# A filter copy and two transpose copies moved between engines, and the last filter products queued earlier, in a tuned FFT-mixing and FFN kernel

## The chip, the cores and the metric

The kernel runs on one core of one Trainium2 chip. The time is device microseconds (us) of one execution. "Span" is the time from the first to the last instruction in the profile, some 2 us shorter. Kernels that are compared were run in the same rounds on the same chip, unless the text says that they come from other rounds. A ratio is the mean time of one kernel's fast runs over that of the other's of the same rounds, so it isn't quite the ratio of the medians that are quoted.

TensorE is PE in the profile, VectorE DVE, ScalarE ACT, GpSimd POOL and SyncE SP.

## The reference

```
batch, seq, dim = 8, 3008, 256
X = rfft(x, axis=1); Y = X * (filt_r + 1j*filt_i); y = irfft(Y)     # per channel: mix along seq
x = y.reshape(24064, 256)
xn = x / rms(x) * rms_g
out = (silu(xn @ w_gate) * (xn @ w_val)) @ w_out                    # d_ff = 1536
```

The program calls one of the eight sequences a "channel". Channel 0 is transformed alone at the start. The other seven are transformed in small pieces between the FFN's matmuls of the channel before.

## The kernel before

Only the filter stage of channel 0, about 17 to 40 us, is concerned. In it 32 frequencies are handled in 16 *units* of two. A unit is a matmul into a PSUM bank (`b_mm`, called `stage_b`), two products with the filter (`b_unit`, called `products`), and the inverse matmuls (`bit_unit`, called `inverses`). Two units form a *pair*: their inverses accumulate in two banks, and the second one ends with two copies to `gT`.

```
# filter tables: four blocks fr[0..3], fi[0..3] of eight frequencies, loaded into half of the
# partitions; f_dup copies the other half: by ScalarE (A), GpSimd (G) or a SyncE transfer (S)
def f_dup(c, e, eng, lo=0, hi=KC):
    t = (fr, fi)[e][c][:, lo:hi, :]
    ...
    if eng is nc.scalar: eng.activation(out=t[a:a + HALF], in_=t[o:o + HALF], func=AXT.Copy)
    elif eng is nc.sync: eng.dma_start(t[a:a + HALF], t[o:o + HALF])
    else:                eng.tensor_copy(out=t[a:a + HALF], in_=t[o:o + HALF])

def t1_copy(g, on_act):          # group g of eight transposes, PSUM -> SBUF
    if on_act: nc.scalar.activation(out=dst, in_=ps[0:KR], func=AXT.Copy)
    else:      nc.vector.tensor_copy(out=dst, in_=ps[0:KR])

def b_unit(b, i, ps):            # products of unit i: VectorE, but units 3, 7, 9, 12 on GpSimd,
    ...                          # after ScalarE has copied the bank to v (GpSimd reads v)

def bit_unit(i):                 # inverses of unit i
    if not closing:
        st[0]["g"][pair] = [bank((3 * dh) if pair == 7 else (1 + dh), "pgt") for dh in range(2)]
    ...                          # 8 matmuls a unit, half of them for each of the two banks
    if closing: ...              # two copies pgt -> gT, mostly by ScalarE

# the schedule; in the traces each engine's instructions stand in this order
for g in range(4):
    t1_mm(g); t1_copy(g, g % 2)
stage_b(0, 1, 2, 3)
for g in range(4, 8): t1_mm(g)
t1_copy(4, 0)
f_dup(0, 0, A, 0, 2); f_dup(0, 1, G, 0, 2); f_dup(0, 0, A, 2, 4); f_dup(0, 1, G, 2, 8)
f_dup(0, 0, A, 4, 8)
products(0) ... products(1) ... t1_copy(5, 1); f_dup(1, 1, G); products(3)
f_dup(1, 0, A, 0, 4); f_dup(1, 0, A, 4, 8)        # "the block-1 copy" below
inverses(0, 1); products(2); t1_copy(6, 0); t1_copy(7, 0)
... # units 4 to 9
inverses(4); products(8); stage_b(12)
inverses(5)
f_dup(3, 1, A, 0, 4); products(12); w_load(0); w_load(1); products(10)
stage_b(13, 14); inverses(6); f_dup(3, 1, A, 4, 8); inverses(7)
... # units 8 to 15, then transposes, norm and FFN
```

Of the kernel before, what the change touches and what calls it, by code (L numbers as in the profile page):

```python
# [121 lines left out]
def kernel(  # L122
# [121 lines left out]
    def b_unit(b, i, ps=None):  # L244
        if ps is None:
            ps = b_mm(b, i)
        f1, f2 = filt(2 * i, 2)
        if b:
            s1 = late_p["sp"].tile([P, 2, D], FP16, tag="s1", name="s1")
            s2 = late_p["sp"].tile([P, 2, D], FP16, tag="s2", name="s2")  # L250
            if summed(b, i):
                nc.vector.tensor_tensor(out=s1, in0=ps, in1=f1, op=ALU.mult)  # L252
                st[b]["s"][i] = (s1, s2, ps, f2)
                return
        elif i % 2:
            s1 = hp.tile([P, 512], FP16, tag="sg", name="sg").rearrange("p (a d) -> p a d", a=2)
            s2 = hhs[(i // 2) % 4].rearrange("p (a d) -> p a d", a=2)
        else:
            ss = xnp.tile([P, 2, 512], FP16, tag="xn", name="ss")
            s1, s2 = (ss[:, e, :].rearrange("p (a d) -> p a d", a=2) for e in range(2))  # L260
        eng = nc.vector
        if (i in (3, 5, 8, 12, 15)) if b else (i in (3, 7, 9, 12)):
            eng = nc.gpsimd
            v = yp.tile([P, 2, 512], FP32, tag="y", name="v")
            v = v[:, 0, :].rearrange("p (a d) -> p a d", a=2)
            nc.scalar.activation(out=v, in_=ps, func=AXT.Copy)
            ps = v
        eng.tensor_tensor(out=s1, in0=ps, in1=f1, op=ALU.mult)
        eng.tensor_tensor(out=s2, in0=ps, in1=f2, op=ALU.mult)  # L269
        st[b]["s"][i] = (s1, s2)  # L270
# [241 lines left out]
    def f_dup(c, e, eng, lo=0, hi=KC):  # L512
        t = (fr, fi)[e][c][:, lo:hi, :]
        a, o = (0, HALF) if e else (HALF, 0)
        if eng is nc.scalar:
            eng.activation(out=t[a:a + HALF], in_=t[o:o + HALF], func=AXT.Copy)  # L516
        elif eng is nc.sync:
            eng.dma_start(t[a:a + HALF], t[o:o + HALF])
        else:
            eng.tensor_copy(out=t[a:a + HALF], in_=t[o:o + HALF])  # L520
# [13 lines left out]
    def t1_mm(g):  # L534
        if g < 6:
            if g % 2 == 0:
                st[0]["t2t"] = t2p.tile([KR, KC, D], FP16, tag="t2", name="t2")
            dst = st[0]["t2t"][:, 4 * (g % 2):4 * (g % 2) + 4, :]
        else:
            dst = t3p.tile([KR, 4, D], FP16, tag="t3", name="t2")  # L540
        st[0]["t2"][g] = dst
        pool, tag = ((psG, "pg"), (psV, "pv"))[g % 2]
        ps = pool.tile([P, 4, D], FP16, tag=tag, name="pt1")
        af = aT.rearrange("p a k -> p (a k)")
        for a in range(4):
            for dh in range(2):
                b0 = dh * H * P
                src = af[:, b0:b0 + 32 * P].rearrange("p (i k) -> p k i", k=K2)[:, 4 * g + a, :]
                nc.tensor.transpose(ps[:, a, ts(dh, P)], src, ident)
        st[0]["t2ps"][g] = ps  # L550

    def t1_copy(g, on_act):
        dst, ps = st[0]["t2"][g], st[0]["t2ps"].pop(g)
        if on_act:
            nc.scalar.activation(out=dst, in_=ps[0:KR], func=AXT.Copy)
        else:
            nc.vector.tensor_copy(out=dst, in_=ps[0:KR])

    def bit_unit(i):
        s1, s2 = st[0]["s"].pop(i)  # L560
        pair = i // 2
        closing = pair in st[0]["g"]
        if not closing:
            st[0]["g"][pair] = [bank((3 * dh) if pair == 7 else (1 + dh), "pgt") for dh in range(2)]
        for u in range(2):
            k = 2 * i + u
            for dh in range(2):
                o = st[0]["g"][pair][dh][:, ts(2 * (i % 2) + u, KR)]
                nc.tensor.matmul(o, s1[:, u, ds(dh * P, P)], wi_at(0, k)[:, 0:KR], start=True, stop=False)
                nc.tensor.matmul(o, s2[:, u, ds(dh * P, P)], wi_at(1, k)[:, 0:KR], start=False, stop=True)  # L570
        if closing:
            for dh in range(2):
                dst = gT[:, dh, pair * 4 * KR:(pair + 1) * 4 * KR]
                src = st[0]["g"][pair][dh][:, 0:4 * KR]
                if pair > 5 and dh:
                    nc.vector.tensor_copy(out=dst, in_=src)
                else:
                    nc.scalar.activation(out=dst, in_=src, func=AXT.Copy)  # L578
# [47 lines left out]
    def w_load(q):  # L626
        cols = ts(q, DFF // 3)
        for src, dst in ((moe_w_gate, wg), (moe_w_val, wv)):
            nc.gpsimd.dma_start(dst[:, :, cols], src.rearrange("(dt p) j -> p dt j", p=P)[:, :, cols])
        nc.gpsimd.dma_start(wo[:, ts(q, JT // 3), :],  # L630
                            moe_w_out.rearrange("(jt p) d -> p jt d", p=P)[:, ts(q, JT // 3), :])

    with tc.manual_schedule():
# [48 lines left out]
        A, G, S = nc.scalar, nc.gpsimd, nc.sync  # L682
        st[0]["t2ps"], st[0]["g"], psb = {}, {}, {}

        def products(*units):
            for i in units:
                b_unit(0, i, psb.pop(i))

        def stage_b(*units):
            for i in units:  # L690
                psb[i] = b_mm(0, i)

        def inverses(*units):
            for i in units:
                bit_unit(i)

        for g in range(4):
            t1_mm(g)
            t1_copy(g, g % 2)
        stage_b(0, 1, 2, 3)  # L700
        for g in range(4, 8):
            t1_mm(g)
        t1_copy(4, 0)
        f_dup(0, 0, A, 0, 2)
        f_dup(0, 1, G, 0, 2)
        f_dup(0, 0, A, 2, 4)
        f_dup(0, 1, G, 2, 8)
        f_dup(0, 0, A, 4, 8)
        products(0)
        stage_b(4)  # L710
        products(1)
# [23 lines left out]
        inverses(4)  # L735
        products(8)
        stage_b(12)
        inverses(5)
        f_dup(3, 1, A, 0, 4)
        products(12)  # L740
        w_load(0)
        w_load(1)
        products(10)
        stage_b(13, 14)
        inverses(6)
# [181 lines left out]
```

## Time and profile before

| | before |
|---|---|
| median time | 889.63 us (three runs, 889.43 to 890.09) |
| span of the profiled run | 886.7 us |
| filter stage | 17.6 to 40.4 us, PE busy 17.60 of 22.80 us |
| start of the block-1 copy on ScalarE | 24.97 us |
| first FFN matmul | 47.20 us |

After the first FFN matmul TensorE has practically no gap (from 110 to 860 us it is busy for 748.86 of 750.00 us).

```profile
47.20 0.38 PE L443 MATMUL pg<-xn,wg 128*128 128x512 f16 x1
```

The line above, from TensorE's instructions in order of time, is the kernel before's first FFN matmul (start, length, line, operation). The prediction shows the other lines.

### The profile page before, as it was taken

To read this page: it belongs to the slowest core of one execution; us is meant where nothing else is said; L and a number is where in the kernel's file an instruction comes from. 1 tells how busy PE (TensorE), PEld (TensorE's weight loads), DVE (VectorE), ACT (ScalarE), POOL (GpSimd) and SP (SyncE) were. 2 spreads that over 40 slices of the span, in tenths; PEclk is the share of its full clock that TensorE was granted. 3 is DMA by queue.
4 is the path that set the end of the run, shared out by engine and by line. 5 is a ranking of instruction groups with operands and counts; after the bars stand their busy time and mean duration, and the time that the engine had idled before them with its cause. 6 is when DMAs were issued, how large, how long until landed. Compare 5 with 4: busy or idle time off the path is not lost.

```text
span 886.7 us, 17463 instructions
## 1 busy us (share of the span) xinstructions
PE 873.2 (98%) x6257; PEld 559.0 (63%) x6257; DVE 678.7 (77%) x1088; ACT 625.3 (71%) x1069; POOL 436.5 (49%) x393
## 2 busy tenths in 40 slices
PE   8799999999999999999999999999999999999998
PEld 5566666666666666666666666666666666666556
DVE  7866786899888877888688887888878887555555
ACT  8878667677677766877677765887667765676444
POOL 7843941646527752667336661376515762155300
PEclk9999999999999999999999999999999999999999
DMA  9595736665653466343736346322352232222202
GB/s 201 118 197 156 163 78 209 143 141 122 177 141 82 101 141 173 93 100 101 193 86 143 85 90 183 93 91 84 99 152 75 64 90 71 77 66 49 72 24 48
DMA packets 80095, 101.44 MB, mean 114 GB/s; under 512 B 8108, under 2 KB 56684, under 8 KB 79560
## 3 DMA queue, kind: packets, MB, share of 16 engines
q1 hardware_dynamic: 69688, 84.23, 34.2%
q0 software_dynamic: 10240, 15.96, 11.5%
q8 instruction: 49, 0.80, 0.4%
q14 instruction: 38, 0.31, 0.1%
q10 hardware_dynamic: 80, 0.13, 0.1%
HBM read 67.67 MB, written 46.78 MB: 129 GB/s over the span
## 4 chain that ended last, share of the span: by engine, by line
PE 93%; DVE 1%; ACT 1%; issue 1%
PE po L462 27%; PE pg L443 27%; PE pv L443 27%; PE psi L291 3%; PE psb L238 3%; PE psn L323 2%; PE psa L203 2%; DVE o L469 1%; PE psq L352 1%; PE pt L589 0%; DVE hh L448 0%; ACT gT L578 0%; ACT fi L516 0%; PE psr L404 0%; PE pw L619 0%
## 5 line engine op out<-in xcount | busy, mean ns | idle before, releaser
L448 DVE TENSOR_TENSOR hh<-pv,sg 128x512 f16<-128x512 f32 (+2 forms) x588 | 392.8, 669 | 189.2 <-ACT sg L447 77.0
L447 ACT ACTIVATE sg<-pg 128x512 f16<-128x512 f32 (+2 forms) x588 | 340.8, 580 | 223.1 <-PE pg L443 213.6
L462 PE MATMUL po<-wo,hh 128*128 128x256 f16 x2244 | 342.6, 273 | 1.2 <-DVE o L469 0.7
L443 PE MATMUL pv<-xn,wv 128*128 128x512 f16 (+2 forms) x1176 | 339.9, 371 | 0.0
L443 PE MATMUL pg<-xn,wg 128*128 128x512 f16 (+2 forms) x1176 | 339.7, 370 | 0.0
L462 PEld LDWEIGHTS <-hh 128*128 128x128 f16 x2256 | 216.2, 97 | 96.8 <-issue 2.6
L282 POOL TENSOR_TENSOR s<-s,s 128x512 f16<-128x512 f16 x101 | 116.6, 1156 | 225.4 <-DVE s L276 156.6
L443 PEld LDWEIGHTS <-wv 128*128 128x128 f16 x1176 | 114.7, 98 | 128.9 <-issue 0.3
L419 POOL TENSOR_TENSOR xn<-y,rb 128x1024 f16<-128x1024 f32 (+1 forms) x45 | 126.1, 2802 | 52.5 <-DMA rb<-r_tmp 44.5
L443 PEld LDWEIGHTS <-wg 128*128 128x128 f16 x1176 | 111.2, 97 | 13.5 <-issue 0.3
L358 POOL TENSOR_TENSOR rho<-u,mhalf 128x4 f32<-128x4 f32 (+1 forms) x48 | 49.0, 1021 | 63.1 <-DVE u L356 62.9
L296 ACT ACTIVATE t<-psi 96x512 f16<-96x512 f32 x112 | 66.3, 592 | 8.3 <-PE psi L291 3.0
L276 DVE TENSOR_TENSOR s<-psb,fi 64x512 f16<-64x512 f32 x101 | 69.0, 683 | 3.0
L278 DVE SCALAR_TENSOR_TENSOR s<-psb,fi 64x512 f16<-64x512 f32 x101 | 69.9, 692 | 1.4
L329 ACT ACTIVATE y<-psn,gsb 128x512 f32<-128x512 f32 (+1 forms) x94 | 63.8, 678 | 7.8 <-PE psn L323 0.5
L252 DVE TENSOR_TENSOR s<-psb,fr 128x512 f16<-128x512 f32 x101 | 68.8, 681 | 0.0
L343 POOL TENSOR_TENSOR sq<-sq 128x512 f16<-128x512 f16 (+1 forms) x35 | 39.6, 1130 | 36.1 <-ACT sq L335 35.2
L335 ACT ACTIVATE sq<-psn 128x512 f16<-128x512 f32 (+1 forms) x94 | 54.8, 583 | 0.0
L208 ACT ACTIVATE t<-psa 128x512 f16<-128x512 f32 x70 | 41.8, 597 | 5.5 <-PE psa L203 2.4
L291 PE MATMUL psi<-s,wi 128*128 128x256 f16 x238 | 44.3, 273 | 0.0
L238 PE MATMUL psb<-t,wb 96*128 96x256 f16 x224 | 43.0, 273 | 0.3 <-DVE s L269 0.2
L323 PEld LDWEIGHTS <-t 128*128 128x128 f16 x368 | 28.3, 98 | 20.6 <-issue 0.4
(104 smaller groups left out, 526.2 us busy)
## 6 DMA issues: line engine op xcount, KB each, us to landing
out_dram<-o SPq DMA_DIRECT2D x83, 256.0 KB
xc<-in_x_dram POOLq DMA_DIRECT2D x56, 192.0 KB, 5.7
z_tmp<-t SPq DMA_DIRECT2D x28, 384.0 KB
t<-z_tmp SPq DMA_DIRECT2D x28, 384.0 KB
g_tmp<-t SPq DMA_DIRECT2D x56, 192.0 KB
rb<-r_tmp SPq DMA_DIRECT2D x41, 256.0 KB
t<-g_tmp SPq DMA_DIRECT2D x21, 384.0 KB
t<-g_tmp SPq DMA_DIRECT2D x7, 320.0 KB
```

The costliest lines, as they stand in the source:

```text
L238: nc.tensor.matmul(ps[:, u, :], w[:, k, :], t, start=True, stop=True)
L252: nc.vector.tensor_tensor(out=s1, in0=ps, in1=f1, op=ALU.mult)
L276: nc.vector.tensor_tensor(out=s2[a], in0=ps[e], in1=f2[e], op=ALU.mult)
L278: nc.vector.scalar_tensor_tensor(out=s2[a], in0=ps[e], scalar=-1.0, in1=f2[e], op0=ALU.mult, op1=ALU.mult)
L282: nc.gpsimd.tensor_tensor(out=s, in0=s1, in1=s2, op=ALU.add)
L291: nc.tensor.matmul(ps[:, u, :], wi_at(q, 2 * i + u), ss[q][:, u, :], start=(q == 0), stop=(q == n - 1))
L296: nc.scalar.activation(out=st[b]["t3"][c][:, 2 * r:2 * r + 2, :], in_=ps[0:KR], func=AXT.Copy)
L419: nc.gpsimd.tensor_tensor(out=xv, in0=yv, in1=rv.unsqueeze(1).to_broadcast([P, 2, n, P]), op=ALU.mult)
L443: nc.tensor.matmul(ps[:, 0:w], wt[:, dt_, ts(jt, P)], xn[:, dt_, :], start=(dt_ == 0), stop=(dt_ == 1))
L447: nc.scalar.activation(out=sg[:, 0:w], in_=pg[:, 0:w], func=AXT.Silu)
L448: nc.vector.tensor_tensor(out=hh[:, 0:w], in0=pv[:, 0:w], in1=sg[:, 0:w], op=ALU.mult)
L462: nc.tensor.matmul(po[s4 // per][:, s4 % per, :], hh[:, ts(s4, P)], wo[:, jt, :], start=(jt == 0 and s4 % per == 0), stop=(jt == JT - 1 an ...
```

## The change

The intent is to take one 64x1024 copy off ScalarE, to let VectorE reach its products sooner, and to have the last block's products ready earlier. The diff, whole:

```
@@ filter stage of channel 0
         for g in range(4):
             t1_mm(g)
-            t1_copy(g, g % 2)
+            t1_copy(g, g == 1)            # (b) copy 3: ScalarE -> VectorE
         stage_b(0, 1, 2, 3)
         for g in range(4, 8):
             t1_mm(g)
-        t1_copy(4, 0)
         f_dup(0, 0, A, 0, 2)
         f_dup(0, 1, G, 0, 2)
         f_dup(0, 0, A, 2, 4)
         f_dup(0, 1, G, 2, 8)
-        f_dup(0, 0, A, 4, 8)
+        t1_copy(4, 1)                     # (b) copy 4: VectorE -> ScalarE
+        f_dup(0, 0, G, 4, 8)              # (a) third piece: ScalarE -> GpSimd
         products(0)
@@
         stage_b(12)
-        inverses(5)
         f_dup(3, 1, A, 0, 4)
         products(12)
         w_load(0)
         w_load(1)
+        inverses(5)                       # (c) unit 12 queued ahead of inverse 5
         products(10)
```

The prediction uses the same letters.

More of the change, by code (lines that the diff above doesn't have):

```diff
@@ L698 @@
             t1_mm(g)
-            t1_copy(g, g % 2)
+            t1_copy(g, g == 1)
         stage_b(0, 1, 2, 3)
@@ L702 @@
             t1_mm(g)
-        t1_copy(4, 0)
         f_dup(0, 0, A, 0, 2)
@@ L707 @@
         f_dup(0, 1, G, 2, 8)
-        f_dup(0, 0, A, 4, 8)
+        t1_copy(4, 1)
+        f_dup(0, 0, G, 4, 8)
         products(0)
@@ L737 @@
         stage_b(12)
-        inverses(5)
         f_dup(3, 1, A, 0, 4)
@@ L742 @@
         w_load(1)
+        inverses(5)
         products(10)
```

## The prediction

> **What bounds the kernel now.** I read the page first, then a table of busy time by stretches of the span, then the chain of work that ended last, then the order in time of each engine between 17 and 48 us.
>
> ```profile
> span 886.7 us, 17463 instructions
> 17.60:40.40 22.80, 17.60 (x239) 14.29 (x238) 18.77 (x32) 18.98 (x30) 19.52 (x18) 1.00 0.54 127
> 40.40:48.20 7.80, 7.56 (x79) 5.50 (x80) 4.97 (x13) 4.57 (x9) 5.59 (x9) 1.00 1.22 181
> 110.00:860.00 750.00, 748.86 (x5146) 473.76 (x5145) 583.65 (x920) 527.53 (x902) 363.92 (x308) 1.00 0.43 109
> ```
>
> The columns after the length are busy us of PE, weight loads, VectorE (DVE), ScalarE (ACT) and GpSimd (POOL). From 110 to 860 us TensorE is busy 748.86 of 750 us: the FFN has no slack, and nothing that the change touches lies there. All that the diff moves lies in the filter stage of channel 0, 17.6 to 40.4 us, where TensorE is busy only 17.60 of 22.80 us. So at most about 5 us are to be had, and what is gained there passes whole to the end, because TensorE merely starts its dense part earlier.
>
> In that stage the chain runs through ScalarE. Its order in time (start, length, line, tiles, idle before):
>
> ```profile
> 24.31 0.58 ACT L266 ACTIVATE v<-psb 128x512 f32<-128x512 f32 x1
> 24.97 2.00 ACT L516 ACTIVATE fr<-fr 64x1024 f32<-64x1024 f32 x2
> 27.00 0.87 ACT L578 ACTIVATE gT<-pgt 128x384 f16<-128x384 f32 x2
> ...
> 31.16 0.60 ACT L266 ACTIVATE v<-psb 128x512 f32<-128x512 f32 x1
> 32.70 0.87 ACT L578 ACTIVATE gT<-pgt 128x384 f16<-128x384 f32 x2 [0.93 <-PE pgt L570]
> 33.59 1.06 ACT L516 ACTIVATE fi<-fi 64x1024 f32<-64x1024 f32 x1
> 34.55 0.57 ACT L266 ACTIVATE v<-psb 128x512 f32<-128x512 f32 x1
> 35.03 1.04 ACT L516 ACTIVATE fi<-fi 64x1024 f32<-64x1024 f32 x1
> 35.97 0.85 ACT L578 ACTIVATE gT<-pgt 128x384 f16<-128x384 f32 x2
> ```
>
> ScalarE works without a gap from 24.97 to 31.76, waits 0.93 us for the inverses of units 4 and 5, and runs gapless to 36.8. TensorE then stands 1.14 us for the copy at 35.97, which gives it a bank for unit 10. From there copies and inverses alternate to the end of the stage at about 39.9. VectorE runs beside this, also gapless:
>
> ```profile
> 19.69 0.69 DVE L557 COPY t<-pt 96x1024 f16<-96x1024 f16 x1 [0.33 <-PE pt L549]
> 21.59 0.69 DVE L557 COPY t<-pt 96x1024 f16<-96x1024 f16 x1 [1.22 <-PE pt L549]
> 22.20 0.68 DVE L268 TENSOR_TENSOR ss<-psb,fr 128x512 f16<-128x512 f32 x1
> ...
> 26.98 0.67 DVE L268 TENSOR_TENSOR ss<-psb,fr 128x512 f16<-128x512 f32 x1
> ...
> 36.17 0.68 DVE L269 TENSOR_TENSOR ss<-psb,fi 128x512 f16<-128x512 f32 x1
> ```
>
> Its first product waits behind the copy of transpose group 4, for which it idled 1.22 us. Unit 4 starts at 26.98, the last product (unit 15) ends at 38.04.
>
> [...] The filter piece is SBUF to SBUF[...]; VectorE's products beside it read PSUM and SBUF, and take 0.68 us in the trace with a GpSimd copy running beside them (22.76 to 24.65) as without.
>
> **Part by part.** The instruction orders of both kernels show that TensorE and the SyncE queue keep their order; ScalarE loses one instruction, GpSimd gains one, VectorE keeps its number.
>
> (a) *Third filter piece (64x1024) to GpSimd.* It takes one 1.06 us instruction off ScalarE. On GpSimd I take half of its 64x2048 copy (1.89 us), 0.95 us, and it falls into a gap:
>
> ```profile
> 19.11 2.03 POOL L520 COPY fi<-fi 64x512 f32<-64x512 f32 x2
> 22.76 1.89 POOL L520 COPY fi<-fi 64x2048 f32<-64x2048 f32 x1 [1.62 <-DMA fi<-in_filt_i_dram]
> 25.03 1.27 POOL L268 TENSOR_TENSOR sg<-v,fr 128x512 f16<-128x512 f32 x1 [0.38 <-DMA fr<-in_filt_r_dram]
> ```
>
> 21.14 + 0.95 = 22.09, before the DMA at 22.7 that GpSimd awaits anyway. Unit 2, its reader, starts at 23.35 below. Free.
>
> (b) *Copies 3 and 4 change engines.* VectorE copies group 3 at 20.3 (TensorE ends it at 20.2), done 20.98, and goes straight to unit 0. The first filter piece is on ScalarE at 20.2 now that copy 3 is gone (its loads have landed by 20.06 in the trace's landing records), done 20.8. So unit 0 starts at about 20.95 in place of 22.20: 1.25 us earlier. Five issues of 0.6 us each later unit 2's second product starts (23.95), then copies 6 and 7, and unit 4 would be reached at 20.95 + 8 x 0.6 = 25.75. ScalarE: pieces one and two to 21.35, copy 4 when TensorE has it (21.6), copy 5 (22.55), the evacuation v of unit 3 at 23.5, ending 24.1, 0.8 earlier.
>
> Here comes **the new wait**. The next work of ScalarE is channel-block 1's filter copy, which needs all three loads of that block. They land at 22.41, 22.85 and 24.81 us; in the queue of SyncE the third shows as an issue held until then:
>
> ```profile
> 23.31 0.77 SPq L503 DMA_DIRECT2D fi<-in_filt_i_dram  x1
> 24.83 2.47 SPq L506 DMA_DIRECT2D fi<-in_filt_i_dram  x2
> ```
>
> No part of the change moves that load. So this copy starts at 24.87, not 24.1: of ScalarE's 0.8 us only 0.1 is left. It ends at 25.9, and unit 4, its reader on VectorE, starts at 25.95: VectorE keeps 1.03 us of its 1.25.
>
> (c) *The last block's products queued ahead of inverse 5.* In ScalarE's order the filter piece (33.59) and v of unit 12 (34.55) go ahead of the gT pair (32.70). The piece's loads have landed by 30.51, and unit 12's matmul follows VectorE's unit 8, now at about 30.9. With the starts of the trace, from 24.87: v of unit 9 ends at 24.87 + 6.79 = 31.66; piece 31.68; v 32.64; gT pair 33.15 (its inverses are done by 31.5, so the 0.93 us wait is gone); second piece 34.04 to 35.08; gT pair of units 6 and 7 at 34.98 in place of 35.97. **Gain 1.0 us**, of which 0.1 is the earlier start and 0.9 the wait.
>
> Do the others keep up? VectorE's unit 14 needs the second piece at 36.17 - 1.03 = 35.14; it ends at 35.08. Unit 15 ends at 37.0 in place of 38.04. GpSimd is fixed at first by the load at 22.76 (ending 24.65): unit 3 at 24.7, not 25.03; the next copy and units 7 and 9 end at 34.15, and unit 12 follows without the 0.69 us wait of today, ending 36.65 in place of 37.70. All three engines gain about 1.0 us, so inverse 15 ends near 38.9 in place of 39.9. The transposes and the first FFN matmul (47.20) follow by a chain of latencies and shift with it: 46.2. Its gate weights land by 41.8, so they do not hold it.
>
> Sum: 889.63 - 1.0 = **888.6 us**.
>
> **The rivals.** *R1, the load at 24.81 does not bind as I think.* If the third load were early, ScalarE would gain the 0.8 us and VectorE its 1.25; then VectorE's last product bounds, gain about 1.25, time 888.4. If it comes later, each 0.1 costs 0.1; the trace speaks for the binding case. *R2, GpSimd becomes the bound.* Its last product ends 36.65 in my sum, only 0.4 us before VectorE's; if the added copy takes twice as long and delays the awaited copy to 23.0, unit 12 ends at 36.9 and the gain is 0.8 (888.8). Against it: 0.67 us of slack in its gap. *R3, gain lost at the changed order.* The gT pair of units 4 and 5 now comes after v; unit 8's inverse needs its bank (34.0, by VectorE's clock it would be ready at 33.8). Worth 0.2 at most, and unit 10 waits until 35.0 anyway. *R4, the whole is hidden*: if what ends the stage were a load rather than engines, the time would stay 889.6. Against it: the chain shows no DMA between 30 and 60 us.
>
> **Range and chances.** Between R2/R3 (0.7 to 0.8) and R1 (1.25) and an uncertainty of the time of about 0.3 (three runs span 889.43 to 890.09): 887.8 to 889.5 us. Two per cent would be 17.8 us, over three times the idle time of TensorE in the stage; there is no mechanism for it either way. Faster 0.005, same 0.99, slower 0.005.
>
> **What would show it.** In the new profile: VectorE's first product near 20.95; ScalarE idle about 0.7 us before the block-1 filter copy, which starts at 24.8 to 25.0; no 0.9 us wait before the gT pair of units 4 and 5; that of units 6 and 7 near 35.0; first FFN matmul near 46.2; everything after it shifted, with busy sums as now. Wrong if the block-1 load lands elsewhere, if VectorE's products lengthen beside GpSimd's copy, or if the first FFN matmul moves by other than 1 us or the later part does not keep the shift.

The lengths are those of the kernel before's trace: on ScalarE 0.62 to 0.64 us for a 64x512 piece, 1.04 to 1.06 for a 64x1024 one and 1.02 for a 96x1024 transpose copy; on VectorE 0.69 us for such a transpose copy, and 0.60 from the start of one product to the next. That GpSimd can make such a filter copy is shown by its own 64x2048 copies, of 1.89 us.

## The result, and the profile after

The changed kernel took 888.25 us in the median (four runs, 887.34 to 888.54), the kernel before 889.53 in the same rounds. The ratio is 0.9983, 95% interval 0.9966 to 1.0: the same within 2%, and about 1.3 us faster by the medians, at the edge of what these few runs can tell.

Here is ScalarE in order of time in the changed kernel, to be held against the lines of the prediction.

```profile
23.18 0.59 ACT L266 ACTIVATE v<-psb 128x512 f32<-128x512 f32 x1
24.33 2.00 ACT L516 ACTIVATE fr<-fr 64x1024 f32<-64x1024 f32 x2 [0.55 <-DMA fr<-in_filt_r_dram]
...
30.53 0.60 ACT L266 ACTIVATE v<-psb 128x512 f32<-128x512 f32 x1
31.16 1.06 ACT L516 ACTIVATE fi<-fi 64x1024 f32<-64x1024 f32 x1
32.12 0.57 ACT L266 ACTIVATE v<-psb 128x512 f32<-128x512 f32 x1
32.60 0.85 ACT L578 ACTIVATE gT<-pgt 128x384 f16<-128x384 f32 x2
33.34 1.05 ACT L516 ACTIVATE fi<-fi 64x1024 f32<-64x1024 f32 x1
34.28 0.85 ACT L578 ACTIVATE gT<-pgt 128x384 f16<-128x384 f32 x2
```

There is the new wait in front of the block-1 copy (0.55 us, for a load), and the 0.93 us wait in front of the gT pair of units 4 and 5 is gone: ScalarE has no gap from 24.33 to the end of the last line. VectorE and GpSimd:

```profile
19.45 1.28 DVE L557 COPY t<-pt 96x1024 f16<-96x1024 f16 x2 [0.32 <-PE pt L549]
20.72 0.69 DVE L268 TENSOR_TENSOR ss<-psb,fr 128x512 f16<-128x512 f32 x1
...
31.43 0.69 DVE L268 TENSOR_TENSOR ss<-psb,fr 128x512 f16<-128x512 f32 x1 [1.06 <-ACT v L266]
```

```profile
20.61 1.06 POOL L520 COPY fr<-fr 64x1024 f32<-64x1024 f32 x1
21.93 1.92 POOL L520 COPY fi<-fi 64x2048 f32<-64x2048 f32 x1 [0.27 <-DMA fi<-in_filt_i_dram]
```

VectorE starts unit 0 at 20.72, as forecast, but stands 1.06 us before unit 10, which was not. GpSimd still waits 0.27 us for its load after the added copy, so part (a) costs nothing there. Four lines of TensorE, in order of time, show what the prediction did not have:

```profile
27.28 0.20 PE L569 MATMUL pgt<-wi,ss 128*128 128x96 f16 x1 [1.92 <-ACT gT L578]
...
29.42 0.64 PE L238 MATMUL psb<-t,wbp 96*128 96x256 f16 x2
...
45.52 0.38 PE L443 MATMUL pg<-xn,wg 128*128 128x512 f16 x1
...
59.65 0.38 PE L203 MATMUL psa<-xc,tb 128*128 128x512 f16 x1 [1.34 <-DMA xc<-in_x_dram]
```

- *A wait for a bank.* In the built program the second accumulator of units 2 and 3 (`pgt`) moved from PSUM bank 3 to bank 2, which the first pair still held. Nobody wrote that: the allocator chooses when the program is built. So TensorE waited 1.92 us for the first pair's copy.
- *Half clock.* The trace's clock record has TensorE at 0.5 from 28.1 to 31.5 us. Two 256-wide matmuls took 0.64 us there; the same pair takes 0.38 elsewhere. The kernel before's profile has no such spell in this stage.
- *The first FFN matmul* came at 45.52, 1.68 us earlier than before. From the block-1 copy the distance is 45.52 - 24.33 = **21.19 us**, 1.04 less than 47.20 - 24.97 = 22.23.
- *The x chunk.* At FFN slot 8 TensorE waited 1.34 us for the first x chunk of channel 1, which it needs 12.63 us after the first FFN matmul (59.83 - 47.20, in the kernel before, where it did not wait). In this one execution that took back most of the 1.68: the last FFN matmul starts at 882.06, against 882.24 before, 0.18 us earlier.

So one profile of each kernel could not say how much the change is worth. The questions were which part gives the 1.04 us, why starts differ from run to run, and whether the x wait is a rule.

### The profile page after: what moved, and what is told of

The parts are those of the page before. It is cut to its first block, busy times and chain, and to the rows that moved or that the text cites. A ratio compares the mean times of both kernels' runs of the same rounds, so it can differ in the third digit from the quotient of the medians.

```text
span 886.6 us, 17467 instructions
## 1 busy us (share of the span) xinstructions
PE 873.1 (98%) x6257; PEld 560.2 (63%) x6257; DVE 679.2 (77%) x1088; ACT 624.5 (70%) x1068; POOL 437.9 (49%) x394
## 4 chain that ended last, share of the span: by engine, by line
PE 88%; DMA 4%; issue 3%; DVE 3%; POOL 1%; ACT 1%; POOLq 0%; SPq 0%
PE po L462 26%; PE pg L443 26%; PE pv L443 25%; PE psb L238 3%; PE psi L291 3%; PE psn L323 2%; PE psa L203 2%; DMA xc<-in_x_dram 1%; DMA fr<-in_filt_r_dram 1%; DVE fr L661 1%; DVE o L469 1%; PE psq L352 0%; ACT gT L578 0%; DMA rb<-r_tmp 0%; DMA r_tmp<-rho 0%
```

## The experiments

Theory: ScalarE's run from the block-1 copy to the first FFN matmul got 1.04 us shorter by (c). Its start shifts with (a) and (b), as far as the load allows. The x wait is a second, later limit. Rivals are named in each expectation.

All outputs were correct. "Distance" is from the start of the block-1 copy to the first FFN matmul, both in that run's profile. The rounds were three (e1 to e4, e5 to e8, e9 to e12), each with the kernel before alongside: medians 889.59, 889.78 and 889.77 us.

| run | copy starts | first FFN matmul | distance | half clock in the stage | median us | ratio, 95% |
|---|---|---|---|---|---|---|
| before (profile) | 24.97 | 47.20 | 22.23 | no | 889.63 | |
| changed (profile) | 24.33 | 45.52 | 21.19 | 28.1 to 31.5 | 888.25 | 0.9983 (0.9966 to 1.0) |
| e1 changed again | 25.50 | 46.69 | 21.19 | 28.7 to 32.1 | 887.63 | 0.9974 (0.9955 to 0.9993) |
| e2 late table | 23.93 | 45.12 | 21.19 | no | 887.97 | 0.998 (0.9957 to 1.0002) |
| e3 before, late table | 26.02 | 49.31 | 23.29 | 30.9 to 37.8 | 889.71 | 1.0007 (0.9984 to 1.0029) |
| e4 banks | 24.10 | 45.94 | 21.84 | no | 888.17 | 0.9979 (0.996 to 0.9998) |
| e5 (c) alone | 24.71 | 45.90 | 21.19 | no | 887.85 | 0.9974 (0.9958 to 0.9991) |
| e6 (a) and (b) | 24.07 | 46.12 | 22.05 | no | 888.57 | 0.9988 (0.9966 to 1.001) |
| e7 x first | 25.73 | 46.91 | 21.18 | no | 888.01 | 0.9973 (0.9956 to 0.999) |
| e8 (b) and (c) | 25.34 | 46.52 | 21.18 | no | 889.03 | 0.9989 (0.997 to 1.0009) |
| e9 SyncE copy | 24.28 | 44.86 | 20.58 | no | 887.11 | 0.9978 (0.996 to 0.9996) |
| e10 before again | 26.36 | 49.58 | 23.22 | 32.5 to 35.9 | 890.62 | 1.0007 (0.9995 to 1.0019) |
| e11 before, fillers | 24.65 | 49.29 | 24.64 | 29.9 to 36.7 | 890.66 | 1.001 (0.9998 to 1.0022) |
| e12 changed, fillers | 25.74 | 47.09 | 21.35 | 25.9 to 29.3 | 889.01 | 0.999 (0.9978 to 1.0002) |

### e1: the changed kernel again

No edit.

> The changed kernel once more, unaltered. Theory (two steps): the filter stage gains 1.0 to 1.7 us, with the spread set by when the third load of channel-block 1 lands (24.2 to 24.8 us), so the first FFN matmul starts between 45.3 and 46.3 us (47.20 before); then TensorE waits for the first x chunk of channel 1 near slot 8 by an amount that differs from run to run (0 to 1.5 us), so the time is 0 to 1.7 us below before, on average about 1.0. Rival (the gain is plain and the 1.34 us wait was a single accident): no x wait at all, time 1.5 us or more below before in every run.

The median was 887.63, 1.96 us under before. The distance was 21.19 again, and there was no x wait: the chunk landed 9.6 us after the first FFN matmul. The load was later, and the copy with it:

```profile
25.50 2.00 ACT L516 ACTIVATE fr<-fr 64x1024 f32<-64x1024 f32 x2 [0.83 <-DVE ss L269]
```

The line names VectorE as what ended the 0.83 us. The landing records have the block's third load at 25.34, so I read it as the load. The x wait differed from run to run, as the theory had it. The rival (no x wait at all) holds for this profile but not for the first, so the wait belongs to some executions only. Two of the theory's numbers were missed: the first FFN matmul, at 46.69, came later than the expected 45.3 to 46.3, because the load landed beyond the range seen until then, and the median lies 1.96 us under before instead of about 1.0.

### e2 and e3: the table load put off

```
-            nc.sync.dma_start(late_p["wb"], tab["wb"])     # in open_late, FFN slot 6
+        at(10, wb_load)                                    # the same load at slot 10
```

> The changed kernel, with the 768 KB load of the second-stage table (hardware queue, issued by SyncE at 48.9 us) put off from FFN slot 6 to slot 10. Theory (that table's packets [...] push the first x chunk of channel 1 back to 59.5): the chunk lands before 57 us, TensorE's 1.34 us wait is gone, and the time is the changed kernel's minus 0.5 to 1.3 us, that is 1.3 to 1.7 us under before. Rival (the software queue alone is late, the table does not matter): the chunk still lands at 58 or later, wait and time unchanged.

> Control: the kernel before with the same put-off table load. The theory says TensorE did not wait for the x chunk there (needed at 59.8, landed 57.7), so the time stays within 0.3 us of before (889.5). If the put-off itself helps elsewhere, it is more than 0.5 us faster.

The chunk of e2 landed at 57.13. No wait showed, but that is 12.0 us after the first FFN matmul, later in those terms than in e1 without the edit. The median, 887.97, is no better than the changed kernel's (887.63 in the same rounds), and its six runs spread from 886.25 to 889.2. The theory that this table's packets delay the chunk is not supported. The control stayed at 889.71, as expected, and its profile brought something else: a half-clock spell, and with it a distance of 23.29 in place of 22.23 (ScalarE waited 1.99 us before the gT pair of units 4 and 5).

### e4: the bank given back

```
-        products(2)
         t1_copy(6, 0)
         t1_copy(7, 0)
+        products(2)
```

> The changed kernel with copies 6 and 7 emitted ahead of the products of unit 2, by which the allocator gives the second pair's second accumulator bank 3 again (in the changed kernel it got bank 2, still held by the first pair, and TensorE stood 1.92 us for its evacuation and then ran 3.4 us at half clock). Theory (ScalarE's chain sets the end of the stage, TensorE's wait is beside it): the 1.9 us wait and the half clock go, VectorE's 1.06 us wait before unit 10 goes, but the first FFN matmul stays where it is in the changed kernel within 0.3 us, and so does the time. Rival (that wait costs the stage): the first FFN matmul is 0.5 to 1 us earlier still.

In the built program the accumulator is in bank 3 again. TensorE's 1.92 us wait, the half clock and VectorE's 1.06 us wait are absent from this profile. The distance was 21.84 because another load came late for ScalarE:

```profile
31.59 1.05 ACT L516 ACTIVATE fi<-fi 64x1024 f32<-64x1024 f32 x1 [0.69 <-DMA fi<-in_filt_i_dram]
```

Without those 0.69 us it would be about 21.2, an estimate. The time, 888.17, is the changed kernel's within the noise. With that estimate TensorE's bank wait did not cost the stage, and the theory holds. The wait isn't needed for a half-clock spell, since e3, e10 and e11 have spells without it; the section on clocks comes back to this.

### e5 and e6: the parts alone

e5 is the kernel before with the last hunk of the diff alone, e6 the changed kernel without that hunk.

> Part (c) alone on the kernel before: the second half-block filter copy and the evacuation of unit 12 ahead of the gT pair of units 4 and 5. Theory: ScalarE runs gapless from the start of the block-1 filter copy to the gT pair of units 6 and 7, so the first FFN matmul comes 21.2 us after the start of that copy (22.23 before, 21.19 in three profiles of the changed kernel); the start itself is not earlier than 24.9. Time 1.0 us under before. Rival (the wait on ScalarE went only because (a) and (b) made VectorE earlier): still 22.0 or more, time as before.

> Parts (a) and (b) alone, ScalarE's order of the last block as before. Theory: VectorE and the block-1 copy may start up to 1.1 us earlier, as far as the third load allows (0 to 1.0 us), and VectorE's earlier unit 8 also shortens ScalarE's 0.93 us wait, as long as TensorE runs at full clock; with a half-clock spell the wait is back at 1 us or more. Distance from copy start to first FFN matmul 21.2 to 22.3; time 0.5 to 1.5 us under before. Rival (all of the gain is (c)): time as before.

ScalarE in e5, in order of time:

```profile
24.71 2.00 ACT L516 ACTIVATE fr<-fr 64x1024 f32<-64x1024 f32 x2
...
30.91 0.60 ACT L266 ACTIVATE v<-psb 128x512 f32<-128x512 f32 x1
31.54 1.05 ACT L516 ACTIVATE fi<-fi 64x1024 f32<-64x1024 f32 x1
32.50 0.57 ACT L266 ACTIVATE v<-psb 128x512 f32<-128x512 f32 x1
32.98 0.84 ACT L578 ACTIVATE gT<-pgt 128x384 f16<-128x384 f32 x2
```

and in e6:

```profile
24.07 2.00 ACT L516 ACTIVATE fr<-fr 64x1024 f32<-64x1024 f32 x2
...
30.26 0.60 ACT L266 ACTIVATE v<-psb 128x512 f32<-128x512 f32 x1
31.62 0.87 ACT L578 ACTIVATE gT<-pgt 128x384 f16<-128x384 f32 x2 [0.75 <-PE pgt L570]
32.51 1.06 ACT L516 ACTIVATE fi<-fi 64x1024 f32<-64x1024 f32 x1
```

This is the clean cut. (c) alone gives the whole 1.04 us of the distance, with VectorE as late as in the kernel before (unit 4 at 26.77; 26.98 there). With (a) and (b) alone ScalarE and VectorE both move about a microsecond earlier (the copy by 0.90, VectorE's unit 4 from 26.98 to 25.90, by 1.08), so the gap between them, which is the wait, hardly shrinks: 0.75 in place of 0.93. What (a) and (b) give is an earlier start when the load is there, as it was in this profile. By time, (c) alone (887.85) cannot be told from the whole change. e6 is 1.2 us under before by the medians, and its interval includes no difference.

### e7: the x chunk ahead of the weights

```
-        w_load(2)
-        for c in range(2):
-            x_load(1, c)
+        x_load(1, 0)
+        w_load(2)
+        x_load(1, 1)
```

> The changed kernel with the first x chunk of channel 1 issued ahead of the last third of the FFN weights. Theory (in the profile of the changed kernel the FFN lost 1.34 us because that chunk landed 14.0 us after the first FFN matmul where it is needed after 12.6): the chunk now lands within 9 us of the first FFN matmul, the wait cannot occur, the weights still come in time, and the median falls by 0.2 to 0.7 us below the changed kernel's, the wait having been in part of the runs alone. Rival (the loads' order does not matter, or the weights become the wait): median unchanged or higher, with a wait of TensorE for wg, wv or wo.

The chunk now landed at 52.23, 5.3 us after the first FFN matmul, so the wait could not occur, and no wait for weights came in its place. The median did not fall: 888.01. The chunk's wait was real in the profiles that have it (1.34 us in the changed kernel, 1.1 in e9, 0.2 in e4), but no gain from taking it away is shown: the changed kernel's two medians are 888.25 and 887.63, in other rounds. How many of the ordinary runs have the wait is not known. My size for it was a miss.

### e8: the third filter piece back on ScalarE

```
         t1_copy(4, 1)
-        f_dup(0, 0, G, 4, 8)
+        f_dup(0, 0, A, 4, 8)
```

> The changed kernel with the third filter piece back on ScalarE, between copies 4 and 5: parts (b) and (c) alone. Theory: ScalarE reaches the block-1 copy about 1.0 us later (24.8 in place of 23.8) but the third load lands between 22.7 and 25.3, so it costs 0 to 1 us, 0.5 on average; the 1.9 us wait of TensorE for a bank goes, as the allocator gives bank 3 again. Time 0.3 to 0.8 us above the changed kernel. Rival (the piece was free on ScalarE, the load binds always): time as the changed kernel's.

The distance is 21.18, unchanged, and the start is 25.34, right behind ScalarE's own earlier work instead of behind a load. The median was 889.03, 0.8 to 1.4 us above the changed kernel's two medians, which come from other rounds. That hints that part (a) is worth something once (b) has put copy 4 on ScalarE, which without (a) carries both. It isn't shown: four of e8's six runs have a lowered mean clock (0.996 to 0.998), and the other two, with spans of 886.1 and 885.7, lie among the changed kernel's. The bank is 3 again here, so (a) is also what tips the allocator.

### e9: towards a faster version

```
         f_dup(3, 1, A, 0, 4)
+        f_dup(3, 1, S, 4, 8)
...
         inverses(6)
-        f_dup(3, 1, A, 4, 8)
```

> Towards a faster version: the changed kernel with the second half of the last block's imaginary filter copy taken off ScalarE and done by a SyncE transfer (issued near 30.6 us, when its loads land; the same kind of transfer for the real half took 4.2 us). Theory (ScalarE's gapless run sets the end): the piece was 0.94 us of that run; the copy lands near 34.8, VectorE needs it at about 35.6 (unit 14), so the distance from the block-1 copy to the first FFN matmul falls from 21.19 to 20.3 to 20.6 and the time by 0.6 to 0.9 us. Rival (the transfer lands late): VectorE waits for it before unit 14 and the distance is 21.0 or more.

```profile
32.55 0.85 ACT L578 ACTIVATE gT<-pgt 128x384 f16<-128x384 f32 x2
33.59 0.87 ACT L578 ACTIVATE gT<-pgt 128x384 f16<-128x384 f32 x2 [0.20 <-PE pgt L570]
```

The two gT pairs now follow each other without the copy between, and the distance fell to 20.58, inside the expected range. The median, 887.11, is the lowest of all kernels. But its runs spread from 885.76 to 891.32, and the ratio (0.9978) is not better than the changed kernel's (0.9974 in e1, other rounds). It beats the kernel before; that it beats the changed kernel in time is not shown. This profile lost 1.1 us to the x wait again; e9 together with e7's order was not run.

### e10, e11 and e12: TensorE's clock and TensorE's load

e10 is the kernel before, unaltered. e11 and e12 add work to TensorE ahead of unit 12:

```
-        if b == 0 and i > 3:
+        for _ in range(0 if b or i < 4 else 6 if i == 12 else 1):
             nc.tensor.matmul(ps[:, 0, :], wz[:, 0:P], wz[:, 0:D], start=True, stop=True)   # filler
```

> The kernel before once more, for its spread: distance from the block-1 copy to the first FFN matmul 22.2 at full TensorE clock, and 23 or more if a half-clock spell falls between 28 and 35 us (23.29 in the one profile with one). Time within 0.3 us of before.

> The kernel before with five more filler matmuls (128x256, 0.107 us each, 0.54 us in all) in front of unit 12's product matmul on TensorE. Theory (in the kernel before TensorE's order puts unit 12 ahead of inverse 5, for which ScalarE's gT pair waits, so TensorE's work there is on the path): distance from the block-1 copy to the first FFN matmul 22.23 + 0.5, about 22.75, and ScalarE's wait before that pair 1.4 to 1.5 us in place of 0.93. Rival (TensorE has slack there): 22.2.

> The changed kernel with the same five fillers. Theory (with the copy and unit 12's evacuation ahead of the pair, ScalarE has other work while TensorE does this): distance still 21.2 within 0.05, time as the changed kernel's. Rival (the order only shifted the wait): 21.7.

e10 had a half-clock spell and a distance of 23.22. ScalarE's wait before the gT pair had doubled, with TensorE as what ended it:

```profile
35.07 0.87 ACT L578 ACTIVATE gT<-pgt 128x384 f16<-128x384 f32 x2 [1.91 <-PE pgt L570]
```

e11 had a longer spell as well, so its 24.64, with a wait of 3.32 us, is not the clean 22.75 that I had asked of it. In the kernel before's trace the matmul behind such a 128x256 one starts 0.108 to 0.121 us after it, so 0.54 us for five was an estimate at full clock. At half clock the five fillers are about 5 x 0.213 = 1.07 us (in e11's trace six of them take 1.28 us, that is 0.213 each). Added to the 23.2 of a spell alone that gives 24.3, an estimate that explains most of 24.64. e12's spell had ended before unit 12. Its distance was 21.35 against 21.19: of 0.54 us of added TensorE work 0.16 arrived. So in these profiles the kernel before passes TensorE's delays on to ScalarE, and the changed order mostly absorbs them. That the spells and fillers overlap in e11 leaves its exact size open. By time, the expectations were not met. e10's median (890.62) lies 0.85 us above before's own (889.77) in the same rounds, where at most 0.3 was expected of an unaltered kernel: a difference of that size between two medians shows nothing by itself. e11 (890.66) is level with e10, and e12 (889.01) is about 1 us slower than the changed kernel was in other rounds; its runs stand 0.8 us under before's median of its own rounds. In e12's profile the first block's loads had ScalarE waiting 2.14 us.

### What the runs' clocks say

Each run records its span and the mean granted clock. The eight profiled runs with no spell in the stage have a mean of 0.999 or 1.000, the six with one 0.995 to 0.998. (The clock also falls to half at the very end of the profile, for the last 0.60 us of the span in the kernel before and 1.75 in the changed one.) Of the kernel before's 33 runs beside the experiments, eight have a clock of 0.999 or more: four spans are 886.5, three 886.6 and one 887.9, mean 886.7. The other 25 range from 887.5 to 892.8. Of the changed kernel's ten runs (both sets) five have it, with spans of 884.9 to 886.3, mean 885.7. The other five have 885.3 to 886.8, mean 886.3. Without spells the change is thus worth 886.7 - 885.7 = 1.0 us, which agrees with the distance's 1.04, though roughly: the changed kernel's five spread over 1.4 us. With spells the changed kernel is at most 886.8 and the kernel before at least 887.5, so the gain is larger. These are sorted runs of several chips, not a controlled experiment, but they agree with the distances of 21.19 against 23.2 in profiles with a spell.

That the changed order absorbs every spell is not shown. The spells profiled in it ended at most 7.15 us after the start of the block-1 copy (31.48 - 24.33), those in the kernel before 9.6 to 12.0 us after it. And e2, which has the same order of the filter stage, has spans of 884.5 and 884.6 in its two runs at 0.999, but 885.4 to 887.4 in its four at 0.997 and 0.998.

What sets off a spell is not shown. In the changed kernel's profile the clock stands at 0.5 from 28.06 to 31.48 us. In the 3.41 us before, 24.65 to 28.06, TensorE was busy for 1.49 us (0.44 of the time), and its bank wait of 1.92 us lies there; e1's, of 2.08 us, likewise ends just before the spell in its profile. So the wait may have brought these two on. But in e2, e6, e7 and e9 there is a bank wait (1.26 us in e6 and e9, 1.3 in e2 and e7) and no spell. Nor does a low busy share alone decide: by their timelines TensorE was busy for about 0.39 of the 3.41 us before the spell in e1 and 0.49 in e10, and in the kernel before's profile there is a stretch of that length with 1.59 us (0.47; 27.30 to 30.71) and no spell in the stage. This is read from profiles whose matmul ends are modelled; no experiment set out to test it.

## Why the prediction was right

The result, 888.25 us, lies in the range of 887.8 to 889.5 and 0.35 us from the 888.6 named. The main term, part (c), was right; that the total came so close is partly luck. In the profiled execution three of the prediction's own signs of being wrong came true: the block-1 load landed elsewhere (24.17), the first FFN matmul moved by 1.68 and not 1, and the later part didn't keep the shift. Point by point:

- **The place and the bound.** Right. Only the filter stage moved, through ScalarE's run.
- **Part (a).** Right. The copy took 1.06 us on GpSimd (0.95 was my half of a longer copy; 1.06 us for 1024 and 1.92 for 2048 elements of the row leave about 0.2 us that does not halve, an estimate) and fitted the gap before the load. VectorE's two products beside it took 0.69 and 0.68 us; in the kernel before they take 0.67 to 0.69.
- **Part (b).** Right. Unit 0 at 20.72 (20.95 forecast), unit 4 at 25.51 (25.95).
- **The new wait.** Right in kind: ScalarE waited for the third load of block 1. The landing was taken as a constant of 24.81 us. In the landing records of the fourteen profiles that load landed between 22.69 and 25.49; in e2 and e6 ScalarE shows no wait for it. Where it waited, the copy started 0.16 us after the landing (24.17 and 24.33, 25.34 and 25.50), as it did before (24.81 and 24.97); the sum had it start at 24.87, 0.06 after. "No part of the change moves that load" is right, but chance moves it by more than the term that I built on it (0.1 us of gain). The first block's loads, which the sum had in time (landed by 20.06), were more often what ScalarE waited for: 0.30 to 2.15 us in six of the eight profiles with (a) and (b).
- **Part (c), 0.9 us from the wait.** Right, and the best confirmed step: 22.23 became 21.19 in the changed kernel and in (c) alone, to 0.01 us.
- **"All three engines gain about 1.0 us".** Half right. VectorE lost 1.06 us before unit 10 in the changed kernel's profile, and it still did not end the stage. So R1's cap was wrong too: with the load 0.64 us early the gain at the first FFN matmul was not held to 1.25 by VectorE but came to 1.68, that is 0.64 of start and 1.04 of (c). TensorE's bank wait of 1.92 us, beside the path, was not foreseen. It comes from the allocator, whose choice the built program shows and the diff doesn't.
- **"What is gained there passes whole to the end".** This step failed in the profiled execution. R4 was set aside because the chain of the kernel before shows no DMA between 30 and 60 us. But the x chunk had landed at 57.69 for a matmul at 59.83, only 2.1 us of slack, and I had not asked what slack the loads after the stage had. In eleven of the fourteen profiles the last FFN matmul starts 835.01 to 835.05 us after the first, so there a gain does pass whole. In the three with an x wait it is 835.37 (e4), 836.46 (e9) and 836.55 us (the changed kernel), so that in the latter 1.50 of 1.68 us were given back, 1.34 of them in the wait itself. It was no rule: e1 has no such wait, and e7, where the chunk landed 5.3 us after the first FFN matmul, has no better median.
- **The size.** 1.0 us was forecast; the medians give 1.28 in the first rounds and 1.96 in e1's. What the sum lacked is TensorE's half-clock spells, which make the kernel before about 1 us longer (23.22 and 23.29 in place of 22.23) and left the changed one at 21.19 in its two profiles with a spell. I had read a profile without a spell, of an execution of 888.58 us, and took its gain from the median of 889.63. The spells raise the gain and the x wait lowers it, neither was in the sum, and what each is worth in the median is not shown.

What stays open: what sets off the half-clock spells, why the x chunk lands between 9.6 and 14.0 us after the first FFN matmul in runs of one and the same program, and how e9 and e7 would do together.

## What to carry to other kernels

When an engine in order waits for another's result while it has later work that is ready, put that work first: here moving one line, with no work saved, gave all of the 1.04 us of the distance. Speeding up both sides of a wait moves the wait and does not remove it: (a) and (b) alone left 0.75 of 0.93 us. Before you call a gain whole, list what the later stages wait for by the clock rather than by the program, above all loads, and how much slack each has; and take a second profile before you treat a load's landing time as a number.
